# Replicated inverse rows in neighbouring partitions: one broadcast load in place of four, with a new late order of issue (RWKV-7 attention into a SwiGLU feed-forward)

## The chip, the cores and the metric

The kernel runs on one core of one Trainium2 chip. The metric is the time of one execution on the device, in microseconds (us). Before the change the median of three runs is 1014.78 us.

## The reference

Two blocks, all in float32. The first is a recurrence over 768 steps for each of 4 x 8 sequences (batch times heads) with a state of 40 x 40; its output is normalized and goes through a gated feed-forward block.

```python
# r, k, v, w, a, b: (4, 8, 768, 40)
for t in range(S):
    y[:, :, t] = einsum('bhd,bhde->bhe', rt, state)
    Sa = einsum('bhde,bhe->bhd', state, at)
    state = state * wt[:, :, None, :] - einsum('bhd,bhe->bhde', Sa, bt) + einsum('bhd,bhe->bhde', vt, kt)
x = y.transpose(0, 2, 1, 3).reshape(3072, 320)          # 8 heads x 40
xn = x / sqrt(mean(x * x, -1) + 1e-6) * rms_g
g = xn @ w_gate                                          # 320 -> 1536
out = (g * sigmoid(g) * (xn @ w_val)) @ w_out            # 1536 -> 320
```

## The kernel before, in words

**Chunks.** The 768 steps are cut into 24 chunks of C = 32. Inside a chunk the recurrence becomes products of matrices and one triangular system per sequence, so that only the state passes from chunk to chunk. 32 sequences (BH = 32) are worked on at once.

**Stages.** For each chunk c the program has:
- `front(c)` (L643): loads w, a, k, b, v of the chunk, transposes them on TensorE, and builds the Gram products (`gramk`) level by level; VectorE places them with predicated copies in LT, the 32 x 32 triangular matrices of all sequences. At its end LT goes to a buffer in DRAM, sB (four DMAs, L747), one row of 32 x 32 = 1024 numbers (4 KB) for each sequence. From sB it is loaded into the tile M (L749, 750) four times, since 128 partitions share the work on 32 sequences.
- `inverse(c)` (L757): VectorE inverts the triangular matrices. A partition holds the whole matrix of one sequence in M and every fourth row of its inverse in Y: partition p works on sequence p % 32 and on the rows 4j + p // 32. Y begins as a copy of the constant eye, those rows of the identity (made at L535 to 538 with a memset and four selects on GpSimd, 32 partitions each). Y goes to the DRAM buffer sY by four DMAs, one for each group of 32 partitions (L788), and from there into LT (four DMAs, L790).
- `main(c)` (L794): the products with the state and with LT, the solve that needs the inverse (`Xs,LT` in the profile), the new state, the scores and levels of the output y, its transposition and normalization.
- `feed(g)` (L930): the feed-forward block for a group of one or two chunks. For each of 12 slices of 128 hidden columns: products with the third, short part of x (64 rows of the array, `64*128` in the profile; kind h64), products with its two long parts (`128*128`, kind hh), the activation on ScalarE, a product on VectorE, and the product with w_out (`po<-wf,hT`, kind out).
- `narrow` (L964) converts the weights, given in float64, on arrival; it is spread over the first part of the run.

**Who does what.** TensorE (PE in the profile; PEld its weight loads) all matmuls and transpositions; VectorE (DVE), ScalarE (ACT) and GpSimd (POOL) the rest. SyncE (SP) issues the DMAs of sB, M, sY, LT, r and the output, POOL most loads of the inputs. All of an engine's instructions and DMA issues stand in one queue and are done in that order.

**The order is written out.** The functions above only record pieces (`Plan.add`, L241): one instruction, or one block of matmuls, each with its engine, and with the pieces that it must follow, worked out from the bytes that it touches (`Plan.foot`, L223). `Plan.issue` (L282) then issues all pieces in the order of the list ORDER (L32 to 183), 5993 numbers: each is the distance of the next piece from the first one not yet issued. So ORDER sets every engine's queue by hand, across chunks and stages: the products of the feed-forward block stand between those of three chunks. PAIRS (L185) says which of three pairs of PSUM banks each piece of work that passes through PSUM uses.

Nearly all instructions carry the line of a helper in the profile (L423 VectorE, L446, L450 and L453 ScalarE, L466 DMA issues, L469 matmuls, L472 transpositions), so they are told apart by their tiles.

Of the kernel before, what the change touches and what calls it, by code (L numbers as in the profile page):

```python
# [7 lines left out]
FP32 = mybir.dt.float32  # L8
I32 = mybir.dt.int32
U32 = mybir.dt.uint32  # L10
AF = mybir.ActivationFunctionType
ALU = mybir.AluOpType
# [4 lines left out]
P = 128  # L17
C = 32
# [324 lines left out]
def kernel(  # L343
# [192 lines left out]
    for m in range(4):  # L536
        e = eye[m * BH:(m + 1) * BH]
        select(e, [[-4, C // 4], [1, C]], -m, 0)
# [508 lines left out]
```

## Time and profile before

| | us |
|---|---|
| median of three runs | 1014.78 |
| lowest and highest run | 1011.59, 1019.46 |
| span of the profiled execution | 1021.8 |
| PE busy | 930.1 (91%) |
| DVE busy | 771.4 (75%) |
| ACT busy | 509.7 (50%) |
| POOL busy | 350.0 (34%) |

Of the profiled execution no other time than its span is given; it is 7.0 us above the median of the runs. All durations below come from it. In rows of a timeline the columns are the start and the length in us, the engine, the line of the program, the operation, what it writes and reads, and the number of instructions merged into the row; a bracket gives the idle time just before and what ended it. In a matmul's row 128*128 is the part of the array that it uses, rows by columns. "SPq" is SyncE's queue issuing a DMA: the row is the issue, not the transfer.

### The profile page before, as it was taken

Reading aid. Unit: us, or ns where it says so; the run is one execution under the profiler, and the core shown is the slowest. Engines: PE = TensorE matmul, PEld = TensorE weight load, DVE = VectorE, ACT = ScalarE, POOL = GpSimd, SP = SyncE. Lnnn points to the kernel's source line nnn. Section 1 sums busy time; section 2 is a strip of 40 time slices with the busy share of each in tenths; the row PEclk is TensorE's granted clock in tenths of the full one; section 3 lists DMA queues with packets and bytes.
Section 4 is the critical chain, followed back from the end, with each engine's and each line's share of the span. In section 5 each row is a group of like instructions: output and inputs, shape, how many; then the busy total and the mean of one; then the engine's idle time right before and its main releaser. Section 6 shows DMA issues by size and latency. Waiting matters only on the chain.

```text
span 1021.8 us, 55373 instructions
## 1 busy us (share of the span) xinstructions
PE 930.1 (91%) x24512; PEld 759.6 (74%) x24512; DVE 771.4 (75%) x2718; ACT 509.7 (50%) x1133; POOL 350.0 (34%) x595
## 2 busy tenths in 40 slices
PE   4366688999989999999999999999999999999998
PEld 4255577878767787788788777778787878788877
DVE  8889877787867966877769779679598697685531
ACT  6788467445445544465353454454544545435121
POOL 8988363242324314315133143143133224210000
PEclk9557767999999999999999999999999999999999
DMA  8574453323324324133232142242232323320100
GB/s 172 149 190 115 96 110 74 68 47 60 54 58 78 56 53 75 36 71 61 45 81 44 44 95 39 55 84 49 43 72 51 75 50 66 67 35 7 43 8 20
DMA packets 140175, 68.87 MB, mean 67 GB/s; under 512 B 120768, under 2 KB 127264, under 8 KB 139936
## 3 DMA queue, kind: packets, MB, share of 16 engines
q0 software_dynamic: 19680, 32.48, 15.9%
q1 hardware_dynamic: 118080, 32.54, 15.4%
q8 instruction: 192, 3.15, 1.3%
q10 hardware_dynamic: 2176, 0.33, 0.2%
q14 instruction: 47, 0.39, 0.1%
HBM read 55.05 MB, written 10.22 MB: 64 GB/s over the span
## 4 chain that ended last, share of the span: by engine, by line
PE 55%; DVE 24%; DMA 7%; issue 5%; POOL 4%; ACT 3%; SPq 2%; DVEq 0%; ACTq 0%; POOLq 0%
PE ps L469 40%; PE po L469 10%; PE ps L472 5%; DVE Yi L423 4%; DVE LT L423 3%; DVE y L423 3%; DVE tmp L423 3%; DVE K L423 3%; DMA sB<-LT 3%; SPq L466 2%; DVE As L423 2%; DMA M<-sB 2%; DVE Ab L423 1%; POOL wf L466 1%; DVE hT L423 1%
## 5 line engine op out<-in xcount | busy, mean ns | idle before, releaser
L469 PE MATMUL ps<-xg,wf 128*128 128x256 f32 (+3 forms) x1872 | 364.5, 377 | 1.5 <-ACT sg L446 0.8
L469 PEld LDWEIGHTS ps<-xg,wf 128*128 128x128 f32 (+1 forms) x1872 | 271.1, 191 | 48.6 <-issue 8.1
L469 PE MATMUL po<-wf,hT 128*128 128x320 f32 x576 | 179.0, 444 | 0.2 <-issue 0.2
L469 PEld LDWEIGHTS po<-wf,hT 128*128 128x128 f32 x576 | 103.5, 189 | 35.6 <-issue 1.4
L423 DVE TENSOR_TENSOR tmp<-Yi,M 128x24 f32<-128x24 f32 (+21 forms) x512 | 107.2, 209 | 12.1 <-DMA M<-sB 1.6
L423 DVE TENSOR_TENSOR Yi<-Yi,tmp 128x24 f32<-128x24 f32 (+21 forms) x512 | 106.8, 209 | 10.4
L423 DVE TENSOR_TENSOR hT<-ps,sg 128x256 f32<-128x256 f32 (+1 forms) x156 | 60.6, 399 | 63.7 <-PE ps L469 41.4
L446 ACT ACTIVATE sg<-ps 128x256 f32<-128x256 f32 (+1 forms) x156 | 54.5, 368 | 103.3 <-PE ps L469 102.4
L466 POOL DMA_DIRECT2D kbn<-in_k_dram x92 | 53.6, 585 | 146.9 <-PE ps L469 146.2
L466 POOL DMA_DIRECT2D kbn<-in_b_dram x92 | 53.8, 587 | 131.2 <-PE ps L469 130.1
L423 DVE TENSOR_TENSOR K<-K,T 128x256 f32<-128x256 f32 (+1 forms) x191 | 92.8, 499 | 3.7 <-PE ps L469 2.8
L469 PE MATMUL ps<-Ab,K 64*60 64x56 f32 (+2 forms) x4608 | 79.4, 224 | 17.5 <-ACT r L450 4.8
L469 PEld LDWEIGHTS ps<-Ab,K 64*60 64x60 f32 (+2 forms) x4608 | 72.6, 136 | 29.0 <-issue 9.3
L423 DVE SCALAR_TENSOR_TENSOR Yi<-M,Yi 128x31 f32<-128x31 f32 (+6 forms) x228 | 43.2, 243 | 66.7 <-DMA out_dram<-o 23.3
L450 ACT COPY KN<-ps 128x640 f32<-128x640 f32 x95 | 65.6, 692 | 46.7 <-PE ps L472 12.9
L466 POOL DMA_DIRECT2D VU<-in_v_dram x92 | 54.1, 590 | 88.0 <-PE ps L469 86.3
L423 DVE TENSOR_TENSOR As<-ps,msi 128x256 f32<-128x256 f32 (+1 forms) x168 | 70.7, 455 | 11.9 <-PE ps L469 7.0
L469 PEld LDWEIGHTS ps<-As,KN 128*40 128x40 f32 x3072 | 67.3, 128 | 15.2 <-issue 5.3
L469 PE MATMUL ps<-As,KN 128*40 128x32 f32 x3072 | 72.0, 208 | 6.1 <-DVE As L423 2.9
L466 POOL DMA_DIRECT2D wn<-in_w_dram x92 | 52.4, 571 | 69.6 <-DVE KN L423 65.4
L450 ACT COPY K<-K 128x512 f32<-128x512 f32 x95 | 60.2, 634 | 23.7 <-PE ps L469 10.9
L456 POOL TENSOR_TENSOR ss<-ss,mhalf 128x1 f32<-128x1 f32 x24 | 18.1, 755 | 147.1 <-DVE ss L423 146.9
(137 smaller groups left out, 1526.4 us busy)
## 6 DMA issues: line engine op xcount, KB each, us to landing
M<-sB SPq DMA_DIRECT2D x96, 128.0 KB, 2.9
wan<-in_r_dram SPq DMA_DIRECT2D x24, 160.0 KB, 4.2
kbn<-in_b_dram POOLq DMA_DIRECT2D x92, 40.0 KB, 2.5
VU<-in_v_dram POOLq DMA_DIRECT2D x92, 40.0 KB, 2.7
wan<-in_w_dram POOLq DMA_DIRECT2D x46, 80.0 KB, 3.0
wan<-in_a_dram POOLq DMA_DIRECT2D x46, 80.0 KB, 2.8
kbn<-in_k_dram POOLq DMA_DIRECT2D x92, 40.0 KB, 2.7
wn<-in_w_dram POOLq DMA_DIRECT2D x92, 40.0 KB, 2.9
```

Of the source, the lines that this page charges most:

```text
L423: plan.add("DVE", time + more + each * size(o), 0.087, lambda at: [fn(at(o), *m(at))], [o], aps(*args))
L446: scalar(o, [a], lambda at: nc.scalar.activation(at(o), at(a), f, **kw), aps(acc), 0.1 if f in (AF.Square, AF.Relu) else 0.0)
L450: scalar(o, [a], lambda at: nc.scalar.copy(at(o), at(a)), extra=more)
L456: plan.add("POOL", 0.5, 0.06, lambda at: nc.gpsimd.tensor_tensor(o, a, b, op), [o], [a, b])
L466: plan.add(by, 0.6 if by == "POOL" else 0.45, 0.0, lambda at: queue.dma_start(out=o, in_=i), [o], [i], load=load, since=since)
L469: return o, lhsT, rhs, lambda at: nc.tensor.matmul(at(o), lhsT, rhs, start=start, stop=stop, skip_group_check=True), 4
L472: return o, i, ident, lambda at: nc.tensor.transpose(at(o), i, ident), 2
```

## The change

- **M by one transfer.** The four copies of a sequence's matrix now stand in four neighbouring partitions: partition p holds sequence p // 4. One DMA of 128 rows of 4 KB reads each row of sB four times, in place of four DMAs of 32 rows.
- **Y and eye** follow: partition p works on the rows 4j + p % 4. Each of the four DMAs to sY takes every fourth partition in place of 32 neighbouring ones. eye is made by an iota of t - 4j on GpSimd, compared on VectorE with p % 4, which comes from a second iota and two small instructions.
- **foot** works out the footprint of an access that steps over partitions.
- **ORDER** has 72 numbers fewer, three for each chunk. On every engine the queue begins as before, with the three M issues taken out: SP's up to its 105th piece, PE's up to its 158th block of 1091, ACT's up to its 287th, DVE's up to its 563rd of 2720 (three instructions for eye added), POOL's up to its 221st. This is the start of the program up to the work on chunks 4 to 6. From there on all queues are in another order, and PAIRS is another list.

```diff
 ORDER = """
-76 84 83 86 75 71 2 3 4 5 6 7 0 35 47 0 17 54 64 0 0 51 0 35 0 55 0 0 67 68 60 190 191 41 49 374 59 71 375 0
...
@@ Plan.foot
-        p, f = divmod(ap.offset, dims[0][0])
+        row = 1
+        for n in ap.tensor.shape[1:]:
+            row *= n
+        p, f = divmod(ap.offset, row)
...
-        return p, p + dims[0][1], self.masks[key]
+        return p, p + (dims[0][1] - 1) * max(dims[0][0] // row, 1) + 1, self.masks[key]
...
@@ the constants
-    blank(eye, 0.0)
-    for m in range(4):
-        e = eye[m * BH:(m + 1) * BH]
-        select(e, [[-4, C // 4], [1, C]], -m, 0)
+    mod = const.tile([P, 2], I32, name="mod")
+    which = mod[:, 1:2].bitcast(FP32)
+    iota(mod[:, 0:1], [[0, 1]], 1)
+    ts(mod[:, 0:1], mod[:, 0:1], 3, None, ALU.bitwise_and)
+    dcopy(which, mod[:, 0:1])
+    ei = eye.bitcast(I32)
+    iota(ei, [[-4, C // 4], [1, C]], 0)
+    ts(eye, ei, which, None, ALU.is_equal)
...
@@ front
         z["M"] = M = M_.next()
-        for m in range(4):
-            dma(M[m * BH:(m + 1) * BH].rearrange("p b x -> p (b x)")[:, 0:C * C], sB, "M")
+        dma(M.rearrange("p b x -> p (b x)")[:, 0:C * C], sB[:, None].to_broadcast((BH, 4, C * C)), "M")
...
@@ inverse
         for m in range(4):
-            dma(sY.rearrange("n (j m t) -> m n j t", m=4, t=C)[m], Y[m * BH:(m + 1) * BH], "sY")
+            dma(sY.rearrange("n (j m t) -> m n j t", m=4, t=C)[m], Y[m:P:4], "sY")
```

More of the change, by code (lines that the diff above doesn't have):

```diff
@@ L32 @@
 ORDER = """
[150 rows of a table removed]
[149 rows of a table added]
 """
 PAIRS = """
-212020210212120201011000000002122102121202002110201212101120120100121021022021021012211022112120021122201112110120220200
-211101012202202011120000200020220222022111222002110010201111111221020101112100110011110120101220200212221202210202000120
-200001010122101111022221020102022012211212111120001012110101122002220000222011120101011110101020010100212121202001201010
-202022202022012001121220211222122020022201202021101121220111201111101001012220112210102111212102000010100200202021210201
-112220222120210
+012020012010102101021011100001020010220212110200010202110021221002100001122012021010121222112121201101021101101102221210
+212222120212202020002020201000000221121220020102111201201221121221221001020111212121010120101012121210222202100020111221
+210111111222011121201000121212210202220020222000102011212121202112121021010201110101000121212101220202102122212220121101
+000200110121212202001020210222020221111010212121020202022200210020200002110101121201201122102020122020210000121020202021
+010112121102102
 """
```

298 rows, old and new, of the table ORDER are left out of this document.

## The prediction

> **What bounds the kernel now.** I read the page's busy shares first, then four stretches of the span.
>
> ```profile
> PE 930.1 (91%) x24512; PEld 759.6 (74%) x24512; DVE 771.4 (75%) x2718; ACT 509.7 (50%) x1133; POOL 350.0 (34%) x595
> ```
>
> ```profile
> 0.00:207.80 207.80, 139.38 (x4944) 123.97 (x4944) 173.29 (x546) 138.73 (x278) 131.86 (x226) 0.75 0.54 121
> 207.80:600.00 392.20, 381.59 (x9894) 306.01 (x9881) 306.76 (x1126) 188.87 (x431) 118.79 (x202) 0.99 0.30 58
> 600.00:1000.00 400.00, 391.93 (x9565) 315.01 (x9564) 288.11 (x1036) 178.67 (x412) 99.36 (x168) 1.00 0.26 52
> 1000.00:1021.80 21.80, 17.24 (x129) 14.59 (x128) 3.22 (x12) 3.42 (x13) 0.00 (x0) 0.98 0.03 8
> ```
>
> The columns are length, busy time of PE, PEld, DVE, ACT and POOL, then granted clock, DMA share and GB/s. The run has two parts. Up to about 208 us PE is idle for 68 us and DVE is the fullest engine (173 of 208). From there to 1000 us PE is idle for 10.6 + 8.1 = 18.7 us of 792, at a granted clock of 0.99 to 1.00. So the late part is as long as PE's queue is, and what a change is worth there is read from how PE's blocks follow one another. A busy PE is not a PE at its peak: the weight loads (PEld) are idle for 171 us of those 792, and the timeline of PEld shows where.
>
> ```profile
> 360.68 0.33 PEld L472 LDWEIGHTS ps<-ident,y 40*128 40x128 f32 x8 [0.44 <-issue]
> 360.89 0.92 PEld L469 LDWEIGHTS ps<-xg,wf 64*128 64x128 f32 x7
> 361.69 0.13 PEld L472 LDWEIGHTS ps<-ident,ST 40*104 40x104 f32 x1
> ...
> 362.65 3.32 PEld L469 LDWEIGHTS ps<-xg,wf 128*128 128x128 f32 x16
> 366.31 0.66 PEld L469 LDWEIGHTS ps<-ST,aP 64*32 64x32 f32 x64 [0.33 <-ACT sg L446]
> 367.01 0.67 PEld L469 LDWEIGHTS ps<-VU,LT 32*32 32x32 f32 x64
> 367.73 0.73 PEld L469 LDWEIGHTS ps<-xg,wf 64*128 64x128 f32 x8
> 368.80 0.67 PEld L469 LDWEIGHTS ps<-Xs,LT 32*32 32x32 f32 x64 [0.33 <-issue]
> ```
>
> ```profile
> 407.10 1.59 PEld L469 LDWEIGHTS ps<-xg,wf 128*128 128x128 f32 x8
> 409.02 0.85 PEld L469 LDWEIGHTS ps<-Xs,LT 32*32 32x32 f32 x64 [0.33 <-issue]
> ...
> 412.06 0.49 PEld L472 LDWEIGHTS ps<-ident,ST 40*104 40x104 f32 x16 [0.33 <-issue]
> 412.47 0.52 PEld L472 LDWEIGHTS ps<-ident,VU 64*104 64x104 f32 x16
> 413.06 0.83 PEld L469 LDWEIGHTS po<-wf,hT 128*128 128x128 f32 x4
> ```
>
> The two numbers with the star are the rows and columns of the array that a block of matmuls uses. When a feed-forward block (xg,wf or wf,hT: 256 or 320 moving columns) is followed by a block of another array size, the next load starts 0.33 to 0.44 us late. A transposition (ident,...) has the 64-row by 128-column shape of the feed's third product (64*128), and between those two there is no gap: the 64*128 block at 360.89 has the transposition behind it after 0.80 us, the one at 367.73 has the solve behind it after 1.07.
>
> **The change, part by part.**
>
> **1. The late order (all of PE's queue from its 159th block, about 208 us).** The counts of blocks are the same in both lists; what moves is who follows whom. I expanded both lists of ORDER and counted, from there to the end, neighbouring blocks whose array sizes differ: 408 stretches of one size before, 395 after. Three prices follow from the rows above.
> - A stretch of 128*128 blocks costs more than its matmuls: 16 loads take 366.31 - 362.65 = 3.66 us to the next block, 8 take 409.02 - 407.10 = 1.92; the 8 more cost 1.74 (0.2175 each), so each stretch has 3.66 - 16 x 0.2175 = 0.18 us on top. There are 151 such stretches before and 140 after: 11 x 0.18 = 2.0 us saved.
> - A 64*128 product followed by another size costs 1.07 - 0.80 = 0.27 more than one followed by its own size. This happens 45 times before and 18 after: 27 x 0.27 = 7.3 us saved. The new list puts these products beside transpositions.
> - A small block followed by another size: a transposition takes 412.47 - 412.06 = 0.41 us to a next one of its size, 413.06 - 412.47 = 0.59 to a 128*128 block, 0.18 more; the state's product shows nothing of it (366.31 + 0.66 to 367.01 is 0.04). 212 of them before, 237 after; with 0.14 for a mean, 25 x 0.14 = 3.5 us lost.
>
> Sum: -2.0 - 7.3 + 3.5 = -5.8 us in PE's queue. The bounds: -9.3 if small blocks pay nothing, -4.8 with the full 0.18 for each; I widen the weak end to -3, since some of the 27 gaps lie under waits.
>
> The Trainium skill, "TensorEngine Tiling (Array Packing)", section Key Properties, says that changing the tiling mode drains TensorE. By that rule alone each of the 13 changes fewer would bring the same 0.33 us, 4.3 us in all; the trace agrees for the blocks with 256 or 320 columns and shows 0.04 us at 367.01, so I keep the sum by rows.
>
> **2. One M transfer for four.** Chunk 23 has no loads beside it:
>
> ```profile
> 946.61 1.71 SPq L466 DMA_DIRECT2D M<-sB  x4
> ```
>
> ```profile
> 947.60:948.60 1.00, 1.00 (x13) 0.89 (x12) 0.55 (x1) 0.00 (x0) 0.00 (x0) 1.00 0.97 275
> 948.60:949.60 1.00, 1.00 (x13) 0.89 (x10) 0.00 (x0) 0.00 (x0) 0.00 (x0) 1.00 0.90 249
> ```
>
> ```profile
> M<-sB SPq DMA_DIRECT2D x96, 128.0 KB, 2.9
> ...
> LT<-sY SPq DMA_DIRECT2D x96, 32.0 KB, 2.8
> ```
>
> Four issues of 0.43 us follow each other on SP, and the 512 KB move in some 2 us with the DMA engines 97% and 90% busy. So the last quarter lands 1.3 us (three issues) + 2.9 = 4.2 us after the first issue. One transfer saves three issues on SP (1.3 us a chunk, for whatever stands behind: sY, LT, the output), but the bytes are the same. No 512 KB transfer is in the trace. At best it lands 2.9 us after its issue, like a quarter: -1.3. At worst its one issue lasts as long as the four (1.71) and the bytes start only then: +1.3. The bytes already fill the engines for most of the time, so I take half of the best, -0.65.
>
> Where this is on the path: the chain of waits holds it in the early part.
>
> ```profile
> 102.93 0.42 SPq L466
> 103.39 3.34 DMA M<-sB
> 107.07 0.65 DVE wf L986
> ```
>
> ```profile
> 203.69 3.34 DMA LT<-sY
> ```
>
> ```profile
> PE ps L469 <- DMA LT<-sY: 1.1, 1, 1.1
> ```
>
> At chunk 2 the end of M is followed at once by DVE: -0.65 (bounds -1.3, +1.3). At 200.48 the four M issues of chunk 5 stand ahead of the LT transfers that end at 207.0 and that PE waits for: -0.65 (bounds -1.3, 0). In chunks 1, 3 and 4 the chain does not pass through M. At chunk 0 it names M ahead of a POOL copy that does not read it; the first product with M comes 3.6 us later, so I take nothing:
>
> ```profile
> 32.52 0.21 DVE L423 TENSOR_TENSOR tmp<-Yi,M 128x30 f32<-128x30 f32 x1
> ```
>
> In the late part M lies under PE's queue, as long as the new list leaves it room (second rival).
>
> **3. Y's four stores** keep count, bytes and their 128-byte runs; only the partition step changes from 1 to 4. I take nothing; bounds +-0.2 us each, hidden with M, the same way.
>
> **4. The identity eye.** A memset and four selects go from POOL, two iotas come; DVE gets three small instructions.
>
> ```profile
> L485 POOL TENSOR_SCALAR_AFFINE_SELECT eye<-eye 32x256 f32<-32x256 f32 x4 | 2.4, 612 | 0.2
> L462 POOL MEMSET eye<- 128x256 f32 x1 | 0.3, 313 | 0.1
> L489 POOL IOTA eye<- 128x32 int32 x2 | 0.3, 162 | 0.0
> L423 DVE TENSOR_SCALAR ss<-ss 128x1 f32<-128x1 f32 x24 | 3.7, 153 | 22.7 <-ACT x L446 22.7
> ```
>
> ```profile
> 27.53 0.74 POOL L466 DMA_DIRECT2D wf<-in_moe_w_gate_dram  x1 [2.46 <-DVE A L423]
> ```
>
> POOL loses 2.7 us and gains 0.16 plus an iota over 128x256, between 0.16 and 8 x 0.162 = 1.3. What it saves ends in the 2.46 us that it waits for DVE at 27.53 anyway: nothing (up to 2.4 us if it did not wait there). DVE gains 0.15 + 0.15 + between 0.15 and 0.5, half a microsecond on the fullest engine of that part: +0.3 (bounds 0, +0.6).
>
> **The sum.** Early: -0.65 - 0.65 + 0.3 = -1.0 (bounds -2.6 to +1.9). Late: -5.8 (-9.3 to -3). Together -6.8 of 1021.8: 1015.0. The profiled execution's span lies above all three runs; the median of the runs is 0.9931 of it, so 1014.8 - 6.8 = **1008.0 us**. Not in this sum is how PE's waits change: other engines' queues are reordered as well. The 18.7 us of PE idle late are the measure; half of them either way, 9.4 us, goes into the range.
>
> **Rivals.**
>
> *Taken back.* DVE is busy 595 of 792 us late, and its work does not shrink; if PE's 5.8 us turn into waits for DVE and ACT, only the early 1.0 is left: 1013.8. For it: the idle of PE is spread over many small waits. Against it: no engine but PE is above 79% there.
>
> *The M chain becomes the bound (slower).* From a chunk's last gram product to the solve that needs LT, PE's queue holds, in the same block times, 46.8 us before and 45.8 after (means of chunks 5 to 23). The chain through sB, M, the inverse, sY and LT must fit in. It is tight in places:
>
> ```profile
> 767.51 1.80 SPq L466 DMA_DIRECT2D LT<-sY  x4
> ```
>
> ```profile
> 771.49 0.79 PE L469 MATMUL ps<-Xs,LT 32*32 32x40 f32 x64
> ```
>
> In chunk 18 the last of four LT issues starts at 768.9 (the row's end less one issue of 0.45) and the solve at 771.5, 2.6 us, about a landing. The last chunk has 976.3 - 971.9 = 4.4:
>
> ```profile
> 970.52 1.80 SPq L466 DMA_DIRECT2D LT<-sY  x4
> ```
>
> ```profile
> 976.31 0.79 PE L469 MATMUL ps<-Xs,LT 32*32 32x40 f32 x64
> ```
>
> Over the 19 chunks, less 2.8 us for the landing, these margins add up so that 1 us less cover and 3 us more for M stall PE by 17 us. That is the point from which it decides. It is reached if the one transfer runs on few DMA engines: on 4 of 16 the 2 us of data become 8, 5.3 us later than now by my estimate, and the margins give 42 us of stalls: about 1050. For it: the source repeats each row four times, a form the trace lacks. Against it: four quarters already keep all engines at 0.97.
>
> The Trainium skill, "DMA: Bandwidth & Descriptors", says in its rules for kernel authors that a leading zero-stride dimension of c copies confines a transfer to c engines; here 32 rows lead and the copies come second, so that by this rule all 16 engines work and the rival falls. No run here shows it.
>
> *The waits go too.* If half of PE's late idle disappears as well: 1008.0 - 9.4 = 998.6. For it: the queues of all engines are new from there on, so that a wait can go as well as come. Against it: DVE's load.
>
> **How the numbers follow.** Forecast 0.58 (own range 1002 to 1013), taken back 0.13, M chain 0.09, waits go 0.20. A difference of 1%, 10.1 us, is about what a measurement can tell here, the three runs lying within 0.8%. Faster by more (below 1004.6): all of the last case and a third of the forecast, 0.20 + 0.20 = 0.40. Slower: the M chain, 0.09. Within: 0.51. The range, 994 to 1020, adds 9.4 us of waits and the bounds of the parts on both sides and leaves the M chain out.
>
> **What would show it.** Right: PE's and PEld's counts as before; late PEld idle smaller by about 6 us, most of it ahead of blocks that follow 64*128; one M issue of 0.4 to 0.7 us per chunk, 512 KB, landing in 3.2 to 4.2 us; the part up to 208 us shorter by about 1 us. Wrong: an M landing above 6 us, PE waiting for LT<-sY in late chunks, or late PE idle away from 18.7 us by more than 9.

## The result and the profile after

The changed kernel takes 1008.92 us (median of 20 runs, 1002.65 to 1014.11), the kernel before 1015.21 (median of 20 runs on the same chip, 1007.99 to 1022.18). The ratio is 0.9941, with a 95% interval of 0.9921 to 0.9961: 6.0 us less, within 1%. The forecast was 1008.0. The total is right, but the terms behind it are not: the experiments show that M's transfer, put at -1.3 us, carries most of the gain, and that the order, put at -5.8 us, carries some 2 us of it.

The profiled executions overstate the difference. Before's span of 1021.8 us lies at the upper end of its runs, after's 1006.5 near the middle of its own, so they differ by 15.3 us where the medians differ by 6.3. A second profile of the kernel after has a span of 1003.0. Differences of a few us between two single profiles are therefore not read as effects below; the ratios decide, and the traces show where.

The busy shares of the kernel after:

```profile
PE 921.0 (92%) x24512; PEld 762.2 (76%) x24512; DVE 777.9 (77%) x2721; ACT 507.1 (50%) x1133; POOL 342.3 (34%) x592
```

Its four stretches (length, busy time of PE, PEld, DVE, ACT, POOL, clock, DMA share, GB/s):

```profile
0.00:207.80 207.80, 143.63 (x5082) 127.59 (x5082) 177.20 (x564) 139.81 (x282) 126.61 (x227) 0.75 0.53 123
207.80:600.00 392.20, 381.85 (x10043) 312.29 (x10035) 313.90 (x1127) 189.49 (x435) 118.21 (x200) 1.00 0.29 59
600.00:985.00 385.00, 378.62 (x9286) 307.89 (x9286) 283.68 (x1021) 174.06 (x403) 97.51 (x165) 1.00 0.25 51
985.00:1006.50 21.50, 16.95 (x127) 14.45 (x125) 3.12 (x12) 3.73 (x13) 0.00 (x0) 1.00 0.10 24
```

The counts of PE and PEld are as before. PE is idle for 10.4 + 6.4 = 16.8 us of the late 777 (18.7 of 792 before) and PEld for 157 (171), some 14 less where the prediction asked for about 6: both queues are shorter, and PE waits about as much. PEld's timeline shows what the new list does. The 64*128 product at 361.96 now stands between two transpositions, and the next load comes 0.79 us later with no gap; the row at 360.15 shows the gap that stays behind 256-column blocks:

```profile
356.50 3.32 PEld L472 LDWEIGHTS ps<-xg,wf 128*128 128x128 f32 x16
360.15 0.66 PEld L472 LDWEIGHTS ps<-ST,aP 64*32 64x32 f32 x64 [0.33 <-issue]
360.86 0.67 PEld L472 LDWEIGHTS ps<-VU,LT 32*32 32x32 f32 x64
361.58 0.49 PEld L475 LDWEIGHTS ps<-ident,ST 40*104 40x104 f32 x16
361.96 0.75 PEld L472 LDWEIGHTS ps<-xg,wf 64*128 64x128 f32 x8
362.75 0.68 PEld L475 LDWEIGHTS ps<-ident,wan 64*104 64x104 f32 x16
363.50 0.67 PEld L472 LDWEIGHTS ps<-Xs,LT 32*32 32x32 f32 x64
```

The one M transfer in the last chunk of the kernel after, SP's timeline first, then two stretches of 1 us:

```profile
931.67 0.56 SPq L469 DMA_DIRECT2D M<-sB  x1
```

```profile
932.70:933.70 1.00, 1.00 (x5) 0.88 (x6) 0.00 (x0) 0.00 (x0) 0.00 (x0) 1.00 0.69 197
933.70:934.70 1.00, 1.00 (x5) 0.70 (x4) 0.00 (x0) 0.00 (x0) 0.00 (x0) 1.00 0.96 340
```

One issue of 0.56 us stands where four took 1.71, and the data move at up to 340 GB/s where the four quarters reached 275. Over all chunks, after's issues of M (ns, minimum, median, maximum) and its landings (us, the same):

```profile
L469 SPq DMA_DIRECT2D M<-sB x24: 537/543/563, 25.8 to 931.7; - x24
DMA to landing us min/median/max: 3.6/4.4/5.5
```

So the issue is as expected (0.4 to 0.7), and the landing of 4.4 lies just above the expected 3.2 to 4.2.

The row that the prediction did not look at stands in the groups of instructions, on DVE. Its columns are busy time, mean ns of one, then idle time of DVE just before the group, and what ended it. From chunk 5 on, the first instruction of each inverse belongs to this group; before, then after:

```profile
L423 DVE SCALAR_TENSOR_TENSOR Yi<-M,Yi 128x31 f32<-128x31 f32 (+6 forms) x228 | 43.2, 243 | 66.7 <-DMA out_dram<-o 23.3 <-DMA M<-sB 21.3 <-DMA LT<-sY 10.0
```

```profile
L426 DVE SCALAR_TENSOR_TENSOR Yi<-M,Yi 128x27 f32<-128x27 f32 (+7 forms) x228 | 46.2, 244 | 53.3 <-DMA M<-sB 21.7 <-DMA LT<-sY 14.9 <-DMA out_dram<-o 5.8
```

Nearly all of this idle time stands ahead of the first instruction of an inverse: 64.5 of the 66.7 us before, 50.2 of the 53.3 after. The three transfers named are those that landed last by the profile, but the instruction itself reads only M and Y. In the kernel after it starts 0.1 to 0.3 us behind M's landing in each of the 15 late chunks whose landing is on record, and in the kernel before in 11 of 19. So it is M that it mostly waits for. DVE works in order: whatever stands behind that instruction in its list (masks, transposed copies, the feed's products) waits too, and PE waits for those. This is the place where M's transfer acts in the late part.

### The profile page after: what moved, and what is told of

Read it like the earlier page. It is cut to its first block, busy times and chain, and to the rows that moved or that the text cites. A ratio compares the mean times of both kernels' runs of the same rounds, so it can differ in the third digit from the quotient of the medians.

```text
span 1006.5 us, 55253 instructions
## 1 busy us (share of the span) xinstructions
PE 921.0 (92%) x24512; PEld 762.2 (76%) x24512; DVE 777.9 (77%) x2721; ACT 507.1 (50%) x1133; POOL 342.3 (34%) x592
## 3 DMA queue, kind: packets, MB, share of 16 engines
q0 software_dynamic: 19680, 32.48, 15.3%
## 4 chain that ended last, share of the span: by engine, by line
PE 69%; DVE 13%; DMA 5%; ACT 5%; issue 3%; SPq 2%; POOL 2%; DVEq 0%; ACTq 0%
PE ps L472 51%; PE po L472 12%; PE ps L475 6%; DVE Yi L426 3%; SPq L469 2%; DVE tmp L426 2%; DMA sB<-LT 1%; DMA LT<-sY 1%; DMA M<-sB 1%; DVE As L426 1%; DVE y L426 1%; DVE LT L426 1%; DVE K L426 1%; ACT VU L453 1%; DMA sY<-Yi 1%
## 5 line engine op out<-in xcount | busy, mean ns | idle before, releaser
L472 PEld LDWEIGHTS ps<-xg,wf 128*128 128x128 f32 (+1 forms) x1872 | 268.3, 189 | 51.6 <-issue 6.2
L426 DVE SCALAR_TENSOR_TENSOR Yi<-M,Yi 128x27 f32<-128x27 f32 (+7 forms) x228 | 46.2, 244 | 53.3 <-DMA M<-sB 21.7
L472 PE MATMUL ps<-As,KN 128*40 128x32 f32 x3072 | 71.3, 207 | 8.6 <-DVE As L426 4.8
```

The lines of the kernel that those rows point to most:

```text
L426: plan.add("DVE", time + more + each * size(o), 0.087, lambda at: [fn(at(o), *m(at))], [o], aps(*args))
L472: return o, lhsT, rhs, lambda at: nc.tensor.matmul(at(o), lhsT, rhs, start=start, stop=stop, skip_group_check=True), 4
```

## The experiments

Each ratio is to the kernel before on the same chip. Two sums from the traces go with them. M's path is the time from the first M issue on SP to DVE's first instruction that reads M, added over chunks 5 to 23. The late stretch runs from PE's 160th block (at 211 to 216 us in all but two) to the start of its last one.

| kernel | late order | M sent as | ratio [95%] | M's path, us | late stretch, us |
|---|---|---|---|---|---|
| before | old | 4 x 128 KB | 1 | 99.6 | 801.9 |
| eye_only | old | 4 x 128 KB | 1.0021 [0.9993, 1.0048] | 99.5 | 795.5 |
| order_only | new | 4 x 128 KB | 0.9996 [0.9968, 1.0025] | 100.0 | 793.0 |
| eye_order | new | 4 x 128 KB | 1.0000 [0.9971, 1.0030] | 104.8 | 798.4 |
| four_m | new | 4 x 128 KB, every 4th partition | 1.0067 [1.0030, 1.0104] | 104.2 | 790.5 |
| change_only | old | 512 KB | 0.9971 [0.9944, 0.9997] | 93.8 | 792.5 |
| after | new | 512 KB | 0.9941 [0.9921, 0.9961] | 90.2 | 790.1 |
| after_again | new | 512 KB | 0.9944 [0.9912, 0.9975] | 90.1 | 785.0 |
| sizes_back | new, 75 changes of size more | 512 KB | 1.0012 [0.9980, 1.0044] | 92.1 | 795.3 |
| m_twice | new | 512 KB behind 512 KB | 1.0339 [1.0295, 1.0384] | 131.0 | 826.7 |
| lead_copies | old | 512 KB, copies leading | 1.1423 [1.1369, 1.1477] | 199.6 | 899.0 |
| m_split | new | 128 + 384 KB | 0.9883 [0.9840, 0.9925] | 71.5 | 783.6 |
| m_split_old | old | 128 + 384 KB | 0.9918 [0.9889, 0.9947] | 71.3 | 786.2 |
| m_split4 | new | 64 + 448 KB | 0.9969 [0.9936, 1.0003] | 75.3 | 784.7 |

(m_twice is counted from the issue of the transfer ahead of M; from M's own issue it is 118.4.) four_m's profiled execution is the fastest of its runs, so its late stretch flatters it. The two profiles of the kernel after differ by 5.1 us in the late stretch, and before and eye_only, whose late parts are the same, by 6.4: a difference of that size between two rows shows nothing by itself.

**The parts alone: order_only, change_only, eye_only, after_again.** The theory at this point was the prediction's: the order is the gain.

order_only is the kernel before with the new ORDER and PAIRS, each M number written as four in a row (728 to 731 in this excerpt); the other early numbers and the eye's places stay, the late ones are those of after's list:

```diff
-805 0 730 796 543 719 47 728 190 192 803 729 722 798 42 731 799 806 43 44
+805 0 796 543 719 47 728 729 730 731 190 192 803 722 798 42 799 806 43 44
...
```

> The kernel before with the new late order alone (four M transfers, old row layout, old eye). Theory A (the gain is PE's queue: fewer changes of array size): ratio to before 0.993 to 0.996, 4 to 7 us less, PE's late queue by block prices 6 us shorter. Rival B (the late order gives nothing, its saving is taken back by waits and the gain comes from the part up to 208 us): 0.998 to 1.002. Rival C (the new order needs the shorter M): above 1.000, with PE waiting for LT<-sY late.

Measured: 0.9996. PE's queue is shorter as worked out: with the lower quartile of each kind of block's pitch, by kind and by whether its neighbours have its array size, the late queue adds up to 766.2 us in the old order and 759.7 in the new. The time does not follow. Theory A fails here.

change_only is the kernel after with the old late list, three of each four M numbers left out, and the old PAIRS; the first numbers that differ:

```diff
-0 350 308 351 352 353 354 355 356 357 399 4 232 233 358 359 0 233 234 408
+0 350 351 399 352 353 232 308 354 0 408 232 3 354 409 355 233 356 234 357
...
```

> The kernel after with the old late order and pairs (one M transfer of 128 rows, new layout, new eye). Theory A: 1 to 3 us less than before, ratio 0.997 to 0.999, with the whole of it before 208 us. Rival B: 4 to 7 us less, ratio 0.993 to 0.996. Chunk 4's solve, at 207.1 us in the profile before and 202.8 after, comes at about 203 to 206 in both.

Measured: 0.9971, 2.9 us less, at the edge of both ranges, and chunk 4's solve at 205.1.

eye_only is the kernel before with the new eye in the old row layout:

```diff
-    blank(eye, 0.0)
-    for m in range(4):
-        e = eye[m * BH:(m + 1) * BH]
-        select(e, [[-4, C // 4], [1, C]], -m, 0)
+    mod = const.tile([P, 2], I32, name="mod")
+    which = mod[:, 1:2].bitcast(FP32)
+    iota(mod[:, 0:1], [[0, 1]], 1)
+    ts(mod[:, 0:1], mod[:, 0:1], 5, None, ALU.logical_shift_right)
+    dcopy(which, mod[:, 0:1])
+    ei = eye.bitcast(I32)
+    iota(ei, [[-4, C // 4], [1, C]], 0)
+    ts(eye, ei, which, None, ALU.is_equal)
```

> The kernel before with the identity eye made by two iotas and a comparison, four M transfers and the old layout kept. As the prediction has it (what POOL saves ends in a wait for DVE): within 0.5 us of before. Rival: the POOL copy at 28.9 us, 3.81 us before and 0.36 after, is what the eye's place decides; then chunk 0's solve comes 1.5 to 2.6 us earlier and the run is 1.5 to 2.5 us shorter, ratio 0.9975 to 0.9985.

Measured: 1.0021, no gain. The POOL copy does follow the eye, and chunk 0's solve comes at 55.5 us in place of 57.4, as the rival had it. POOL's timeline before, and in eye_only:

```profile
27.53 0.74 POOL L466 DMA_DIRECT2D wf<-in_moe_w_gate_dram  x1 [2.46 <-DVE A L423]
28.26 0.54 POOL L462 MEMSET LT<- 128x512 f32 x1
28.86 3.81 POOL L459 COPY msi<-msk 64x16 f32<-64x16 f32 x1
```

```profile
27.03 0.74 POOL L503 DMA_DIRECT2D wf<-in_moe_w_gate_dram  x1 [4.52 <-DVE A L460]
27.76 0.56 POOL L499 MEMSET LT<- 128x512 f32 x1
28.27 0.36 POOL L496 COPY msi<-msk 64x16 f32<-64x16 f32 x1
```

POOL's saving goes into the wait for DVE, 2.46 before and 4.52 here, as the prediction said; the copy behind it then takes 0.36 us in place of 3.81. It does so in every kernel profiled with the new eye, and takes 3.80 to 3.89 in every one with the old. Chunk 4's solve comes at 207.1 and 208.1 with the old eye and four M transfers, at 205.5 to 207.4 with the new eye and four (three kernels): about 1 us earlier, and not to be seen in the time.

after_again is the kernel after, unchanged.

> The kernel after once more, on the chip of the three parts: ratio 0.992 to 0.996 as measured before. If the parts add, order alone and layout alone together give this ratio within 0.002. Its profile shows how far two profiles of one kernel differ: within 5 us if the 15.3 us between the two profiles is the change, up to 9 us if most of the excess over the 6.3 us of the medians is the draw.

Measured: 0.9944, with a span of 1003.0, 3.5 us from the first profile's. The parts do add within their intervals (0.9996 and 0.9971 give 0.9967), but the sum is short of the whole by 0.0023 to 0.0026: the parts may need each other.

**What M's transfer is worth: eye_order, four_m.** eye_order is order_only with the eye of eye_only; it lacks the layout and the one transfer alone.

> The kernel before with the new eye and the new late order, four M transfers and the old layout kept: what it lacks of the kernel after is M's one transfer. Theory A (order worth 3 to 6 us by PE's queue, eye 2 us, M 1 us): ratio 0.993 to 0.996. Rival B (the order's gain needs the one transfer, as its 0.9996 without it suggests): 0.998 to 1.001, and M's transfer then carries 4 us or more.

Measured: 1.0000. Rival B holds: without M's one transfer the order and the eye bring nothing that can be measured. four_m is the kernel after with the M transfer alone undone:

```diff
-        dma(M.rearrange("p b x -> p (b x)")[:, 0:C * C], sB[:, None].to_broadcast((BH, 4, C * C)), "M")
+        for m in range(4):
+            dma(M[m:P:4].rearrange("p b x -> p (b x)")[:, 0:C * C], sB, "M")
```

> The kernel after with M's transfer alone undone: four transfers of 32 rows again, each to every fourth partition; the new row layout, Y's stores, eye and order stay. Theory A (M's one transfer is the gain, by 0.45 us less of DVE's standing in each late chunk): DVE's wait at M in chunks 5 to 23 goes from 45 to 50 us back to 58 to 66, ratio to before 0.998 to 1.001. Rival (the layout's other effects, Y's stores or the eye, carry it): 0.993 to 0.996.

Measured: 1.0067, more than theory A asked. DVE's idle time at M is back at 61.8 us, as theory A had it. In the five kernels with four transfers that idle time is 60.9 to 67.6 us, in the four with one transfer, the rows leading and nothing sent ahead of it, 45.3 to 58.9. four_m's issues are dearer. SP's row for M before, and in four_m:

```profile
L466 SPq DMA_DIRECT2D M<-sB x96: 308/421/1447, 25.9 to 947.9; - x96
```

```profile
L523 SPq DMA_DIRECT2D M<-sB x96: 491/593/1718, 26.1 to 938.6; - x96
```

Four issues of 0.593 us to every fourth partition take 2.4 us, four of 0.421 to neighbouring ones 1.7. M's path is no longer for it than in eye_order (104.2 against 104.8), so why four_m is slower than eye_order (1.0000) stays open. Either way the layout, Y's stores, the eye and the order do not carry the gain by themselves. With one transfer in place of four, the ratio falls by 0.0050 in the old order (eye_only to change_only), by 0.0056 to 0.0059 in the new (eye_order to after_again and after) and by 0.0126 where the four are strided.

**The M path made longer: lead_copies, m_twice.** lead_copies is the kernel before with one M transfer in the old layout:

```diff
-        for m in range(4):
-            dma(M[m * BH:(m + 1) * BH].rearrange("p b x -> p (b x)")[:, 0:C * C], sB, "M")
+        dma(M.rearrange("p b x -> p (b x)")[:, 0:C * C], sB[None].to_broadcast((4, BH, C * C)), "M")
```

> The kernel before with one M transfer in the old row layout: the four copies lead and the 32 rows come second; order, pairs and eye as before. Theory A (any one transfer of 512 KB spreads over all engines): landing 4 to 5 us as in the kernel after, ratio 0.997 to 1.000. Rival (the slower one of the prediction: leading copies confine it to 4 of the 16 engines): landing 8 to 11 us, PE waiting for LT<-sY late, 1030 to 1055 us, ratio 1.015 to 1.04.

Measured: 1.1423, 1160 us: far beyond the rival's own range. M's landing is not on record in this profile, so the transfer is read from the DMA engines. Stretches of 1 us while the last M moves, then DVE's group:

```profile
1083.00:1084.00 1.00, 1.00 (x6) 0.90 (x5) 0.00 (x0) 0.00 (x0) 0.00 (x0) 1.00 0.22 70
1084.00:1085.00 1.00, 1.00 (x7) 0.87 (x6) 0.00 (x0) 0.38 (x1) 0.00 (x0) 1.00 0.25 94
1085.00:1086.00 1.00, 1.00 (x6) 0.88 (x5) 0.00 (x0) 0.00 (x0) 0.00 (x0) 1.00 0.25 98
```

```profile
L458 DVE SCALAR_TENSOR_TENSOR Yi<-M,Yi 128x31 f32<-128x31 f32 (+6 forms) x228 | 43.2, 243 | 166.5 <-DMA M<-sB 86.4 <-DMA out_dram<-o 38.3 <-DMA LT<-sY 28.6
```

A DMA share of 0.22 to 0.25 at 70 to 98 GB/s is what 4 of 16 engines give, against 0.96 and 340 GB/s in the kernel after: the same bytes, and of the transfer only the order of two dimensions differs. The Trainium skill, "DMA: Bandwidth & Descriptors", rules for kernel authors, says that a leading broadcast of c copies confines a transfer to at most c engines. This run agrees with it (a share of 0.25 with four copies leading), and so does the kernel after, where the rows lead (0.96). M's path is 199.6 - 99.6 = 100 us longer than with four quarters, 5.3 a chunk, the prediction's own estimate. But the late stretch grows by 899.0 - 798.7 (mean of before and eye_only) = 100 us, as much as the path. Some 40 us more come ahead of it: the late stretch starts at 254 us, in before and eye_only at 214 and 212.

m_twice leaves nothing out and sends the source once more, to a place in DRAM that nothing reads, ahead of M:

```diff
+    M2 = dram.tile([BH, 4, C * C], FP32, name="M2")
...
-        dma(M.rearrange("p b x -> p (b x)")[:, 0:C * C], sB[:, None].to_broadcast((BH, 4, C * C)), "M")
+        Mo, Mi = M.rearrange("p b x -> p (b x)")[:, 0:C * C], sB[:, None].to_broadcast((BH, 4, C * C))
+        plan.add("SP", 0.9, 0.0, lambda at, Mo=Mo, Mi=Mi: [nc.sync.dma_start(out=M2, in_=Mi),
+                                                          nc.sync.dma_start(out=Mo, in_=Mi)], [Mo], [Mi], load="M")
```

> The kernel after with 512 KB more ahead of each M: the same source is first sent to a place in DRAM that nothing reads, so that M comes about 2 us later (0.5 us of issue and up to 2 us of data). Theory A (M decides only in chunks 0 to 4, where the chain holds it; late it is covered): chunk 4's solve 4 to 8 us later and the late part 0 to 6 us longer, ratio 0.998 to 1.008 to before. Rival B (the M chain is near deciding in the late part too): the late part 8 to 20 us longer with PE waiting for LT<-sY, ratio 1.008 to 1.025.

Measured: 1.0339. M's path grows by 131.0 - 90.2 = 41 us, the late stretch by 826.7 - 787.6 (mean of the two profiles of after) = 39, beyond rival B's range. The profile is of the slowest of the kernel's six runs. By the ratios the whole run is 40 us longer, and 8 of these lie ahead of the late stretch, so the late part's share is 32 to 39. The transfer ahead also delays what SP issues behind it and moves 512 KB more a chunk; lead_copies does neither, and its late stretch grows as much as its path too.

Not all of this is waiting. The late stretch as one window, with the columns of the four stretches above, in before, after, m_twice and lead_copies:

```profile
214.30:1016.20 801.90, 783.45 (x19399) 630.56 (x19396) 592.69 (x2149) 366.65 (x845) 215.71 (x365) 0.99 0.28 54
211.20:1001.30 790.10, 773.37 (x19407) 631.73 (x19402) 597.87 (x2146) 365.12 (x846) 215.72 (x365) 1.00 0.27 54
220.20:1046.90 826.70, 788.39 (x19407) 641.96 (x19404) 597.67 (x2146) 366.03 (x846) 215.77 (x365) 0.98 0.29 63
253.60:1152.60 899.00, 814.20 (x19400) 653.50 (x19397) 592.84 (x2149) 367.60 (x845) 215.78 (x365) 0.94 0.24 48
```

PE is idle (length less busy time) for 16.7 us in the kernel after and 38.3 in m_twice, and its busy time for the same work rises from 773.4 to 788.4. Against the mean of the two profiles of after, m_twice's 39 us are 24 of waiting and 15 of a slower PE; lead_copies' 100 us, against the mean of before and eye_only, are 68 and 33. The busy time rises where the granted clock falls: it is 0.98 and 0.94 here, 0.99 to 1.00 in the others. The profile grants PE half its clock for 38 us of m_twice's late stretch and for 99 us of lead_copies', for 3 us in the kernel after. Each of these 24 half-clock stretches in the two longer kernels comes straight behind 3.4 us in which PE was idle for at least 1.5. Not every such wait is followed by one, and no run changes the clock alone. So a long wait of PE can come with a cost beyond its own length.

PE does not wait for LT for most of its idle time. PE's waits (total us, times, longest) in m_twice, then the same rows of the kernel after:

```profile
PE ps L522 <- issue: 17.9, 14, 3.7
PE ps L525 <- DVE y L476: 8.7, 4, 4.6
PE ps L522 <- DVE hT L476: 8.3, 5, 4.0
...
PE ps L522 <- DMA LT<-sY: 6.6, 5, 2.2
```

```profile
PE ps L472 <- issue: 10.2, 10, 2.6
PE ps L475 <- DVE y L426: 8.5, 5, 3.4
...
PE ps L472 <- DVE hT L426: 2.0, 2, 1.3
```

Waits for LT are 6.6 us in all; the rest of the idle time is spread over what DVE does behind the inverse, hT of the feed among it (8.3 against 2.0), and over waits that the profile cannot name. DVE's group stands for 91.8 us, against 53.3 and 47.9 in the two profiles of the kernel after:

```profile
L476 DVE SCALAR_TENSOR_TENSOR Yi<-M,Yi 128x27 f32<-128x27 f32 (+7 forms) x228 | 46.2, 244 | 91.8 <-DMA M<-sB 31.7 <-DMA LT<-sY 30.1 <-issue 18.3
```

**The price of a change of array size: sizes_back.** The kernel after, with 65 exchanges in PE's late list, for example:

```diff
-  feed 1, piece 6 (128*128) | feed 1, piece 5 (128*128) | chunk 4, piece 35 (another size)
+  feed 1, piece 6 (128*128) | chunk 4, piece 35 (another size) | feed 1, piece 5 (128*128)
```

> The kernel after with 65 exchanges of neighbouring blocks in PE's late list, chosen where both blocks had their data and their users had time, so that neighbours of different array size rise from 394 to 469 (64*128 products followed by another size from 18 to 25). Theory A (a change of size costs what the prediction's block prices say, and the end moves with PE's queue): the pitches of the blocks make the queue 14.6 us longer, so about 1023 us, ratio to before 1.006 to 1.010. Theory B (waits give back half of what PE's queue gains or loses): 7 us longer, 1.000 to 1.003. Theory C (no such price): as the kernel after, 0.993 to 0.997.

Measured: 1.0012 against 0.9941 for the kernel after: 7.2 us, with an uncertainty of some 4, for 14.6 us of queue. That is theory B, half of it. The price of a block itself is as predicted. In the kernel after, a 64*128 product followed by its own size takes 0.755 us to the next block (53 of them), one followed by another size 1.064 (18): 0.31 for the 0.27 of the prediction.

**The M path made shorter: m_split, m_split_old, m_split4.** The inverse uses M's rows in order, so the first rows can go ahead. m_split is the kernel after with

```diff
-        dma(M.rearrange("p b x -> p (b x)")[:, 0:C * C], sB[:, None].to_broadcast((BH, 4, C * C)), "M")
+        cuts = (0, C) if c < BLOCKED else (0, 8, C)
+        for s0, s1 in zip(cuts, cuts[1:]):
+            dma(M.rearrange("p b x -> p (b x)")[:, s0 * C:s1 * C], sB[:, None, s0 * C:s1 * C].to_broadcast((BH, 4, (s1 - s0) * C)), "M")
```

and two M pieces in ORDER where one was. m_split_old has the old late list, m_split4 has `(0, 4, C)`.

> The kernel after with M sent in two transfers from chunk 5 on: rows 0 to 7 of each matrix first (128 KB), rows 8 to 31 behind them (384 KB); the inverse uses the rows in that order. Its first instruction then waits for a 128 KB landing (2.9 to 3.1 us) in place of a 512 KB one (4.4). Theory A (DVE stands at M in every late chunk and what stands there passes to the end one for one, as the 2.1 us a chunk of the doubled transfer did with 40 us): 1.0 to 1.5 us less in 19 chunks, 19 to 28 us, less what PE's queue holds back: 982 to 996 us, ratio to before 0.967 to 0.981. Theory B (M is covered late by PE's queue, as the prediction had it): within 2 us of the kernel after, 0.992 to 0.997.

> The same two transfers with the old late order and pairs. If PE's shorter queue in the new order is hidden by DVE's wait for M, it shows once that wait is shorter: 4 to 8 us more than the new order with the same transfers. If the new order is worth nothing of itself: within 2 us of it.

> The kernel after with rows 0 to 3 first (64 KB), rows 4 to 31 behind them (448 KB). By theory A the first instruction starts 0 to 0.3 us earlier than with 8 rows, while row 4 is needed some 1 us after the start and its transfer lands 1.0 to 1.5 us after the first: 0 to 5 us more than with 8 rows. By theory B no difference.

Measured: m_split 0.9883 (1004.81 us), the fastest kernel here, 5.9 us less than the kernel after. The transfers of m_split (KB each, median us to landing), and its DVE group:

```profile
M<-sB SPq DMA_DIRECT2D x19, 384.0 KB, 4.5
...
M<-sB SPq DMA_DIRECT2D x19, 128.0 KB, 3.1
```

```profile
L477 DVE SCALAR_TENSOR_TENSOR Yi<-M,Yi 128x27 f32<-128x27 f32 (+7 forms) x228 | 46.1, 243 | 30.6 <-DMA M<-sB 22.2 <-ACT Yi L504 5.0
```

M's path is 18.7 us shorter and DVE stands 17 to 23 us less, as theory A had it, but the run gains 6 us and not 19 to 28. So M's path comes out nearly in full only when it gets longer. When it gets shorter, little is left to gain: in the kernel after PE is idle for 12.6 to 16.7 us of the late stretch and the clock is full, and in m_split PE is busy for 770.5 us of the late 783.6. m_split_old lies 0.0035 above m_split, 3.6 us, just below its range of 4 to 8. m_split4 lies 0.0086 above m_split, more than the 0 to 5 us expected. Its small first part gains nothing at the start (M's path 75.3). Its ratio of 0.9969 is no better than the kernel after's, though its path is 15 us shorter; why is open. DVE stands at M 17 times, and 8 times in m_split, whose row comes second:

```profile
DVE Yi L477 <- DMA M<-sB: 30.8, 17, 6.7
```

```profile
DVE Yi L477 <- DMA M<-sB: 22.2, 8, 5.1
```

## Why the prediction was right in its sum and wrong in its terms

**The late order, -5.8 us.** The working on PE's queue holds: 0.31 us measured for the 0.27 of a 64*128 product, and 6.5 us less queue by the blocks' pitches. PE's busy time in the late stretch agrees: 776.5 to 783.5 us in the four kernels with the old order whose M is not delayed, 770.5 to 773.8 in the seven with the new list as it stands. What failed is the step behind it, "the late part is as long as PE's queue is". From the old order to the new, the time falls by 0.4 us (before to order_only), 2.1 (eye_only to eye_order), 2.7 to 3.0 (change_only to the two runs of after) and 3.6 (m_split_old to m_split). Each alone lies within its uncertainty of some 4 to 5 us; the mean is 2.2 to 2.3, itself uncertain by some 2 us, and sizes_back puts the rate at half from the other side. So the "taken back" rival, given 0.13, holds for about half of the term or more. The traces show it too: from m_split_old to m_split, both at a granted clock of 1.00, PE's late busy time falls from 776.5 to 770.5 us and its idle time rises from 9.7 to 13.1. PE is busy 98% of the late part and still waits often enough that it can't keep what its queue saves.

**M's transfer, -0.65 us twice, nothing late.** The size was nearly right: M's path is 99.6 - 90.2 = 9.4 us shorter in 19 chunks, 0.5 a chunk for the 0.65. The place was wrong. "In the late part M lies under PE's queue" was reckoned from PE's side alone, from a chunk's gram product to the solve that needs LT. That margin is there: PE waits little for LT. But M is first awaited by DVE, whose inverse stands at it in most late chunks, and everything behind that instruction in DVE's list is late with it. The prediction did not ask what is queued behind DVE's waiting instruction, though the row with 66.7 us of idle time stood in the profile of before. The one transfer is worth 5 to 6 us where eye and order are held and the four go to neighbouring rows.

**The early part, -1.0 us.** Chunk 4's solve comes at 207.1 and 208.1 us with the old eye and four transfers, at 205.5 to 207.4 with the new eye, and at 202.8 to 208.1 in the seven profiles with the whole early change: means of 207.6, 206.6 and 205.4. That is 2.2 us, inside the bounds of -2.6 to +1.9, but kernels of one kind differ by up to 5.3. By these means about half comes with the eye, put at +0.3, though eye_only's time shows no gain (1.0021): POOL's saving ended in its wait for DVE as said, but a copy behind that wait got 3.45 us shorter, which the prediction had not counted.

**Y's stores, 0.** Their landing is 2.4 us after and 2.6 before. They were not changed alone; four_m has them in the new form and gains nothing.

**The M chain as the bound, 0.09.** The mechanism and its engines were right: 4 of 16, and 5.3 us a chunk. Its price was not: 1160 us measured, 1050 worked out, with 100 us in the late stretch for the 42 of stalls. "That is the point from which it decides", 3 us, came from PE's margins. On DVE's side it decides sooner: 2.2 us a chunk (41 / 19) cost 40 us of the run. Nor did the sum of margins have a term for the clock, which fell with PE's waits (0.94). It did not come about here only because the rows lead in the changed transfer.

**The sum.** -1.0 and -5.8 were forecast; about -2 with the eye and the early chunks (by chunk 4's solve), -2 from the order and some -3 from M in the late part would make up the 6 measured. These three come from different comparisons with intervals of 3 us and more, so the split is rough. That terms so far off add up to within 1 us of the forecast is luck. But that M's one transfer is needed for the gain is shown (eye_order, four_m), and so is that the order alone doesn't make it (order_only). What stays open is which of DVE's instructions behind the inverse passes the wait on to PE: the profile ends 17.9 us of PE's waits in m_twice with no releaser.

## What to carry to other kernels

A transfer's cover has to be read on the engine that waits for it first, in order, and not on the busiest engine: ask what stands behind the waiting instruction. An engine at 98% is still not the only bound; a shorter queue there was worth about half its length in time, and a wait on another engine that grew came out nearly in full, part of it because PE's granted clock fell as PE stood. Shortened, the same wait gave a third (18.7 us gave 6). In a broadcast transfer, put the rows ahead of the copies; where the reader uses the data in order, sending the first part alone can pay: 128 KB of 512 did here, 64 KB did not.

## What the runs showed of the hardware that was not expected

- One broadcast of 512 KB with the rows leading lands in 4.4 us (median) and moves at up to 340 GB/s; with four copies leading it runs at a DMA share of 0.25 and 94 to 98 GB/s.
- One issue costs SP 0.543 us for 128 rows, 0.421 for 32 neighbouring partitions, 0.593 for every fourth of 128.
- PE's granted clock falls to half for 3.4 to 10.2 us behind waits: 38 us of m_twice's late stretch, 99 of lead_copies', each time straight behind 3.4 us with at least 1.5 of idle time.
- The POOL copy of 64x16 took 3.81 us before and 0.36 after. Its start does not decide: in eye_order it starts at 28.81, within 0.05 us of before's 28.86, and takes 0.36; in lead_copies it starts at 28.05 and takes 3.80. In the long case DVE was working mostly on products of two tensors, in the short one on operations of one tensor with a constant or a column:

```profile
28.51 0.68 DVE L423 TENSOR_TENSOR K<-K,T 128x512 f32<-128x512 f32 x1
29.11 0.44 DVE L423 TENSOR_TENSOR Ab<-A,T 128x192 f32<-128x192 f32 x1
```

```profile
27.05 0.66 DVE L426 TENSOR_SCALAR eye<-eye,mod 128x256 f32<-128x256 int32 x1
27.63 0.80 DVE L426 TENSOR_SCALAR exs<-wf 128x480 int32<-128x480 int32 x1
```

  The first fence is DVE's timeline before, the second after, where the copy starts at 28.11. The Trainium skill, "GPSIMD Engine Reference", section Key points, names contention with DVE instructions in a 2-port performance mode or with two inputs in SBUF. The rows with two inputs fit it, and no run here changed that alone.
